# Windowed attention and routed experts on one core: the transfers of rows a step later, the splits of W2's sums one by one, table operations out of five products

## The chip, the core and the metric

The kernel runs on one core of one Trainium2 chip. The metric is device time in microseconds (us): the median of several executions of the whole program. One execution was also recorded by the hardware profiler. Its record, the trace, gives the start and length of every instruction on the core's engines, and all rows quoted here are from it. The engines are TensorE (PE; its weight loads are PEld), VectorE (DVE), ScalarE (ACT), GpSimd (POOL) and SyncE (SP, which issues most DMAs). Each works through its own instructions in order; semaphores hold an instruction until what it reads or overwrites is ready.

## What is computed

Attention over 8 batches, 8 heads, 576 positions and 64 dimensions, where each position sees itself and the 63 before it; then a mixture of 8 experts, of which each of the 4608 tokens takes the one with the largest logit:

```python
scores = np.matmul(q, k.transpose(0, 1, 3, 2)) / np.sqrt(64)
scores = np.where((rel >= 0) & (rel < 64), scores, -1e9)      # rel = row - column
attn = softmax(scores)
x = (attn @ v).transpose(0, 2, 1, 3).reshape(4608, 512)
logits = x @ w_gate + modality_bias[modality_id]
e_idx, gate_w = argmax(logits), max(softmax(logits))
for e in range(8):
    h = np.maximum(x[e_idx == e] @ w1[e], 0.0)                # 512 to 1024
    out[e_idx == e] = gate_w * (h @ w2[e])                    # 1024 to 512
```

## The kernel before

All loops are unrolled and the order of the instructions of every engine is written by hand: what the Python code issues first, an engine runs first.

**Steps.** The attention works on 36 pairs of blocks of 64 positions, 128 rows of x each. A loop over steps `s` (line 1211) runs 40 steps as a pipeline: step s computes the scores of pair s (`scores`, L748, on TensorE; `minima`, L765, the masked scores and their minimum per row on DVE; `exps`, L777, on ScalarE), turns the probabilities of pair s-1 (`probs_t`), multiplies pair s-2 with the values (`values`, L803; `values_out`, L811, which writes the pair's rows into a buffer `xa`) and takes the logits of pair s-3 (`logits`, L828, L833). A pair's own values and those of the block before it lie in different partitions, so `swap_v` puts a copy `ve` together: its upper half by DVE (L678), its lower by POOL (L679). POOL also adds a small number to the sums of the exponentials (`sums`, `rs`, L792), and in steps 6 to 11 makes the first half of a weight's split (`high`, L113).

**Rows.** Two pairs make a group G. In step 2G + 5, an odd one, `route2` and `route3` work out where each of the group's 256 tokens goes in a scratch memory that is sorted by expert. Small DVE operations wait in a list `routing`; `tick(n)` issues the next n of that list and then of a second list, `queue`, which holds table operations (on one partition, a few elements each: where an expert's rows begin, which experts are processed when). The last entry of `routing` is `rows`: a cast of the targets to integers (L916) and, for each of the two pairs, `scatter`: a POOL copy of the tokens' numbers into the last column of `xa` (L903) and an indirect DMA of the 128 rows of 514 numbers (L904). There are five `xa` buffers: pair p uses number p modulo 5. In steps 0 to 11 each step has ticks of 2, 6 and 6, from step 12 on of 2, 5 and 5. So up to step 11 the six entries behind `route3` all fit into the odd step's last tick; from step 12 on `rows` is left over, and runs at the next, even step's first tick, which stands behind that step's `swap_v`, `sums` and the transposes of x.

**Slots.** From step 12 on, pieces of the experts' work on TensorE stand between the parts of a step, and after step 39 they run alone. A slot is 256 tokens of one expert (`fetch` loads them from scratch into `xt`, L203; `x_part` turns them, L266, and splits them into `xh` and `xl`, L194 and L195). Numbers of 32 bits are split into a high and a low part, hi on ScalarE and lo on DVE, and three products are taken. From the eighth slot on, slots are "fast": the product with W2 takes seven half-size products P1 to P7 of sums and differences of its quarters (L387), in the order P1, P7, P2, P4, P5, P6, P3, with the first product's pieces (L291) between them.

**Sums of W2.** For this, `combine` (L1176, four POOL operations) makes the sums of two loaded pieces of W2, and `sums_parts` splits them (`put_parts`, L1179 on ScalarE and L1180 on DVE), three splits for the first expert, in steps 16 to 19, two for the second, in steps 36 to 39. `combine` runs in the middle of the step, behind `swap_v`; `sums_parts` at its end; the next pieces are loaded behind it (`sums_load`).

**After step 39** a loop (line 1509) issues the remaining pieces one by one and, after each, `tick(3)` until the table `rows2` is done and then `tick(1)`, as well as loads and splits of further weights.

Of the kernel before, what the change touches and what calls it, by code (L numbers as in the profile page):

```python
# [26 lines left out]
def tile_window_attn_moe(  # L27
# [12 lines left out]
    nc = tc.nc  # L40
    B, H, S, D = q.shape
    N = B * S
    DM = H * D
# [19 lines left out]
    FIRST = 12  # L63
# [144 lines left out]

    todo = []
    last = []  # L210
    position = [-4]
    pads = []
    RAWS = 8
# [22 lines left out]
    def run_later():  # L236
        while later:
            later.pop(0)()
# [14 lines left out]
    def slot_pieces():  # L253
# [157 lines left out]
        def fast_step(sl, nm):  # L411

            product(sl, nm, *dict(
                p1=("a11", "b11"), p7=("s3", "t3"), p2=("a12", "b21"), p4=("a22", "t4"),
                p5=("s1", "t1"), p6=("s2", "t2"), p3=("s4", "b22"))[nm])
            later.append(lambda: fast_out(sl, nm))
# [96 lines left out]
        while True:  # L513
            nxt = None
            if sl["fast"]:
                for k in (1, 2):
                    for i in range(2):
                        first(sl, k, i)
                        yield
                fast_step(sl, "p1")  # L520
                run_after()
                yield
                first(sl, 3, 0)
                yield
                nxt = fetch()
                first(sl, 3, 1)
                yield
                fast_step(sl, "p7")
                run_after()
                yield  # L530
                fast_step(sl, "p2")
                run_after()
                later.append(lambda: rest_of(sl, "s2"))
                yield
                fast_step(sl, "p4")
                later.append(lambda: rest_of(sl, "s4"))
                yield
                x_part(nxt, 0)
                run_later()
                x_part(nxt, 1)  # L540
                run_later()
                fast_step(sl, "p5")
                yield
                fast_step(sl, "p6")
                yield
                first(nxt, 0, 0)
                yield
                first(nxt, 0, 1)
                yield
                fast_step(sl, "p3")  # L550
                yield
                sl = nxt
                continue
            for k in range(1, NK):
                for i in range(2):
                    if k == 2 and i == 1:
                        assert todo
                        nxt = fetch()
                    first(sl, k, i)
                    yield  # L560
                for t in range(2):
                    second(sl, k - 1, t)
                    if k == NK - 1 and nxt and t == 1:
                        x_part(nxt, 1)
                    yield
                    if k == NK - 1 and nxt and t == 0:
                        x_part(nxt, 0)
                        run_later()
            second(sl, NK - 1, 0)
            yield  # L570
            if nxt["nb"] == 1:
                break
            first(nxt, 0, 0)
            yield
            first(nxt, 0, 1)
            yield
            second(sl, NK - 1, 1)
            yield
            sl = nxt
# [227 lines left out]
    def values_out(p):  # L807
        rs = st.pop((p, "rs"))
        nc.vector.reciprocal(out=rs, in_=rs)
        xa = st[p, "xa"] = xas[p % XBUF]  # L810
        nc.vector.tensor_tensor(  # L811
            out=xa[:, 0:DM].rearrange("p (h d) -> p h d", d=D), in0=st.pop((p, "av")),
            in1=rs[:, :, None].broadcast_to([P, H, D]), op=ALU.mult)

    def x_t(p, xp):
        xa = st[p, "xa"]
# [63 lines left out]
    def route3(G, rk):  # L880

        ex, oh = st.pop((G, "r")), chosen.pop(G)
        xg = [st.pop((GB * G + j, "xa")) for j in range(GB)]
        tgt = small.tile(sh3, F32, name="tgt")
        nc.vector.tensor_tensor(
            out=tgt, in0=rk.rearrange("p (j e) -> p j e", e=E), in1=ebase, op=ALU.add)
        se = small.tile([P, GB], F32, name="se")
        dst = small.tile([P, GB], F32, name="dst")
        idx = small.tile([P, GB], I32, name="idx")
        routing.append(lambda: nc.vector.reduce_sum(out=se, in_=ex, axis=AX.X))  # L890
        routing.append(lambda: nc.vector.tensor_tensor(out=tgt, in0=tgt, in1=oh[:, 1:], op=ALU.mult))
        routing.append(lambda: nc.vector.tensor_scalar(
            out=se, in0=se, scalar1=1e-9, scalar2=None, op0=ALU.add))
        routing.append(lambda: nc.vector.reduce_sum(out=dst, in_=tgt, axis=AX.X))

        def gates():
            for j in range(GB):
                nc.vector.reciprocal(out=xg[j][:, DM:DM + 1], in_=se[:, j:j + 1])
        routing.append(gates)

        def scatter(j):
            p = GB * G + j
            nc.gpsimd.tensor_copy(out=xg[j][:, DM + 1:DM + 2], in_=idc[:, p:p + 1])  # L903
            ins = nc.gpsimd.indirect_dma_start(  # L904
                out=xs, out_offset=bass.IndirectOffsetOnAxis(ap=idx[:, j:j + 1], axis=0),
                in_=xg[j], in_offset=None)
            tc.declare_no_dep(ins.ins, group="scatter", reason="rows are distinct")
            tc.add_to_no_dep_group("scatter", ins.ins)
            late = [T for T, _ in EARLY if T < G]
            if late:  # L910
                tc.declare_no_dep(ins.ins, group="early_loads", reason="rows read are older")
            for T in late:
                tc.add_to_no_dep_group(f"scatter_after_{T}", ins.ins)

        def rows():
            nc.vector.tensor_copy(out=idx, in_=dst)  # L916
            for j in range(GB):
                scatter(j)
            scattered.append(f"scatter_after_{G}")
        routing.append(rows)  # L920
# [257 lines left out]
    def put_parts(src, hi, lo):  # L1178
        nc.scalar.copy(out=hi, in_=src)  # L1179
        nc.vector.tensor_tensor(out=lo, in0=src, in1=hi.bitcast(F32), op=ALU.subtract)  # L1180
# [10 lines left out]
    def sums_load(x, j):  # L1191
# [2 lines left out]
            mixed[0][:, i * 512:(i + 1) * 512] for i in (2 * (j % 2), 2 * (j % 2) + 1)]  # L1194
        sums_x[x, j] = [load_piece(r, evs[x], 8 + j + 4 * i) for i, r in enumerate(raw)]

    def sums_parts(x, j):

        a, b = sums_x.pop((x, j))
        f13, f2 = combos[x][0:2]  # L1200
        put_parts(a, f13[0][:, j, :], f13[1][:, j, :])
        put_parts(b[:, half:DM], f2[0][:, j, :], f2[1][:, j, :])
        if not x:
            f4 = combos[x][2]
            put_parts(b[:, 0:half], f4[0][:, j, :], f4[1][:, j, :])

    combos = {}
    SUMS = {FIRST + 4 + j: (0, j) for j in range(4)}
# [2 lines left out]
    for s in range(NPR + 4):  # L1211
# [17 lines left out]
                       for _ in range(2)]))  # L1229
        for f, args in at.pop(s, ()):  # L1230
            f(*args)
        n_tick = 6 if s < FIRST else 5
        n_gap = 0 if s < FIRST else 4
        heads = list(parts[s])
        R = (s - 5) // GB if s >= 5 and j == 1 else -1
# [26 lines left out]
            high(s)  # L1262
        if s in SUMS:
            combine(*sums_x[SUMS[s]])
        if s < NPR:
            exps(s, (0, 1))
        if n_gap > 0 and s != FIRST:
# [3 lines left out]
        if 2 <= s < NPR + 2:  # L1271
            x_t(s - 2, turn_bank(s))
        run_later()
        tick(2)
        if s < NPR:
            exps(s, (2, 3, 4))
# [5 lines left out]
        if heads:  # L1282
            some_heads(s, *heads.pop(0), nc.vector.tensor_copy)
        run_later()
        tick(n_tick)
        cnt = None
        if R >= 0:
# [15 lines left out]
        while heads:  # L1303
# [2 lines left out]
                s, G, part, nc.scalar.copy if part in (K1, K0) or s < FIRST and (G, part) != (1, Q0) else  # L1306
                nc.vector.tensor_copy)
        run_later()
        tick(n_tick)
        if s >= 4:  # L1310
            weights(s)
        if s in SUMS:
            sums_parts(*SUMS[s])
        if s + 1 in SUMS:
            sums_load(*SUMS[s + 1])
        if n_gap > 3:
# [192 lines left out]
    while next(it, "end") != "end":  # L1509
        run_later()  # L1510
        t = position[0]
        waited += 1
        tick(3 if issued[0] < ready2 else 1)
        if len(pads) > E + 1:
            if t > begin_of[slot_y - 2]:
                pad_rows(pads.pop(0))
        elif len(pads) > E:
            if not todo or todo[0][2] != 0 or todo[0][1] is not None:
                pad_rows(pads.pop(0))
        elif pads and t >= begin_of[slot_y] + 16 and waited % 4 == 0:  # L1520
            tick(ready_i - issued[0], table=True)
            pad_rows(pads.pop(0))
        while n_load < len(loads) and loads[n_load][0] <= t + RAWS and (
                n_load < RAWS or loads[n_load - RAWS][3] < n_task):
            _, c, ev, _ = loads[n_load]
            raw_of[n_load] = load_piece(raw_tile(), ev(), c)
            n_load += 1
        if n_task < len(tasks) and tasks[n_task][0] <= t:
            _, f, ids = tasks[n_task]
            f(*(raw_of[i] for i in ids))  # L1530
            n_task += 1
# [125 lines left out]
```

## Time and profile before

| | us |
|---|---|
| median of 3 runs | 635.52 |
| lowest, highest | 634.42, 636.5 |
| the profiled execution | 640.02 |
| its span, first to last instruction | 638.2 |

The mean clock that TensorE was granted is 0.995 of full speed. In the profile, a row of the timeline gives an instruction's start and length in us, engine, line, operation, result and operands with their sizes, and, in brackets, how long the engine was idle before it and what ended that. `x32` means 32 such instructions merged into one row. `DVE xl L195` in a wait is the instruction of line 195 on DVE that writes `xl`. The step's number can be told from line 811, which each step has once: it begins step 7 at 53.68 us, step 9 at 65.50 and step 11 at 78.06.

### The profile page before, as it was taken

The page shows a single profiled execution, that of the slowest core. Times are in us where ns is not written, and L with a number is a line of the kernel's source. Part 1 is how long each engine was busy: PE and PEld are TensorE (multiplying, and loading weights), DVE is VectorE, ACT ScalarE, POOL GpSimd, SP SyncE. Part 2 cuts the span into 40 slices and gives each one's busy share as a digit, 9 for nine tenths or more (in the row PEclk, how much of TensorE's full clock was granted, in tenths as well). Part 3 has the DMA queues.
Part 4 walks back from the last instruction along what each step waited for, and adds up shares of the span by engine and source line. Part 5 has one row for each costly group of instructions (what it writes and reads, how often), then busy time and mean ns, then how long its engine had stood idle before and what let it go on. Part 6 is the DMA issues. An engine that isn't in the chain of part 4 may idle for free.

```text
span 638.2 us, 18317 instructions
## 1 busy us (share of the span) xinstructions
PE 611.9 (96%) x6831; PEld 567.1 (89%) x6831; DVE 431.9 (68%) x1645; ACT 340.4 (53%) x1049; POOL 177.1 (28%) x365
## 2 busy tenths in 40 slices
PE   6998889999999999999999989999999999999996
PEld 4887779888898989898988979999999999999885
DVE  2778967777757676666554567698667766675752
ACT  3799876666665656455644233463544454244541
POOL 5315431355232222320324650262111001101112
PEclk9999989999999999999999999999999999999999
DMA  9999884763754564534323347014773102505630
GB/s 178 194 186 244 217 226 124 207 191 85 199 166 123 151 160 134 140 79 115 102 78 115 97 156 236 34 49 133 238 243 117 51 34 67 181 18 187 210 118 35
DMA packets 141035, 89.71 MB, mean 141 GB/s; under 512 B 118858, under 2 KB 118896, under 8 KB 140784
## 3 DMA queue, kind: packets, MB, share of 16 engines
q1 hardware_dynamic: 132256, 69.02, 42.1%
q0 software_dynamic: 5856, 18.92, 7.8%
q8 instruction: 54, 0.88, 0.6%
q10 hardware_dynamic: 2832, 0.59, 0.5%
q14 instruction: 37, 0.30, 0.2%
HBM read 69.06 MB, written 24.96 MB: 147 GB/s over the span
## 4 chain that ended last, share of the span: by engine, by line
PE 55%; DVE 6%; DMA 1%; issue 1%; ACT 1%; POOL 1%; POOLq 0%; SPq 0%; DVEq 0%; ACTq 0%
PE em L291 14%; PE sp L291 9%; PE y L428 9%; PE y L387 7%; PE tp L608 4%; PE sp L387 3%; PE av L803 2%; PE sp L748 2%; PE av L387 2%; PE y L482 1%; PE tp L828 1%; DVE M L1180 1%; DVE y L407 1%; DMA vo<-in_moe_w_dram 1%; PE tp L266 1%
## 5 line engine op out<-in xcount | busy, mean ns | idle before, releaser
L777 ACT ACTIVATE ss<-ss,mn 128x128 f32<-128x128 f32 x240 | 94.1, 398 | 2.6 <-DVE mn L765 2.6
L442 POOL DMA_INDIRECT out_dram<-y,id x36 | 36.6, 1016 | 207.8 <-DVE y L407 114.4
L428 PE MATMUL y<-M,hh 128*128 128x512 f32 x256 | 83.6, 408 | 0.0
L291 PE MATMUL em<-xh,M 128*128 128x256 f32 x544 | 80.3, 290 | 2.4 <-DVE xl L195 2.4
L786 ACT COPY pT<-tp 128x512 f32<-128x512 f32 x59 | 32.5, 590 | 79.2 <-PE tp L608 78.1
L291 PEld LDWEIGHTS em<-xh,M 128*128 128x128 f32 x544 | 69.4, 191 | 3.3 <-DVE xl L195 3.1
L765 DVE CUSTOM_DVE_ANT_0 ss<-sp,masks 128x128 f32<-128x128 f32 x240 | 53.6, 287 | 19.6 <-PE sp L748 15.5
L904 POOL DMA_INDIRECT xs_scratch<-xa,idx x36 | 36.3, 1009 | 64.7 <-DVE rows L141 30.8
L428 PE MATMUL y<-M,hl 128*128 128x512 f32 x128 | 50.3, 393 | 0.0
L803 PEld LDWEIGHTS av<-ve,pT 128*64 128x64 f32 x576 | 36.3, 138 | 15.8 <-issue 9.5
L428 PEld LDWEIGHTS y<-M,hh 128*128 128x128 f32 x256 | 43.8, 188 | 6.0
L803 PE MATMUL av<-ve,pT 128*64 128x64 f32 x576 | 41.0, 225 | 6.5 <-DVE ve L678 3.3
L304 DVE SCALAR_TENSOR_TENSOR hl<-em,hh 128x512 fp32r<-128x512 f32 x32 | 22.1, 691 | 37.1 <-ACT hh L303 32.2
L777 ACT ACTIVATION_READ_ACCUMULATOR ss<-ss,mn 128x1 f32 x240 | 46.4, 193 | 0.0
L748 PE MATMUL sp<-kT,qT 64*64 64x128 f32 x1152 | 42.0, 284 | 2.2 <-DVE qT L731 0.8
L291 PE MATMUL em<-xl,M 128*128 128x256 f32 x272 | 43.4, 282 | 0.0
L291 PEld LDWEIGHTS em<-xl,M 128*128 128x128 f32 x272 | 37.0, 190 | 0.0
L291 PE MATMUL em<-xh,S 128*128 128x256 f32 x256 | 35.4, 280 | 0.8 <-DVE xl L195 0.7
L748 PEld LDWEIGHTS sp<-kT,qT 64*64 64x64 f32 x1152 | 32.5, 137 | 3.8 <-ACT qT L714 1.2
L291 PE MATMUL sp<-xh,S 128*128 128x256 f32 x256 | 35.2, 279 | 0.0
L803 PE MATMUL av<-vo,pT 128*64 128x64 f32 x480 | 34.4, 225 | 0.0
L608 PE MATMUL tp<-ident_r,ss 128*128 128x128 f32 x220 | 32.2, 284 | 1.8 <-DVE lg L833 1.8
(341 smaller groups left out, 1608.1 us busy)
## 6 DMA issues: line engine op xcount, KB each, us to landing
xt<-xs_scratch SPq DMA_DIRECT2D x18, 514.0 KB
vo<-in_v_dram SPq DMA_DIRECT2D x27, 256.0 KB
vo<-in_moe_w_dram SPq DMA_DIRECT2D x25, 256.0 KB
ss<-in_moe_w_dram SPq DMA_DIRECT2D x25, 256.0 KB
y<-in_moe_w_dram SPq DMA_DIRECT2D x24, 256.0 KB
xs_scratch<-xs_scratch SPq DMA_DIRECT2D x10, 514.0 KB
qk<-in_q_dram SPq DMA_DIRECT2D x16, 256.0 KB
qk<-in_k_dram SPq DMA_DIRECT2D x16, 256.0 KB
```

The source lines that it names most:

```text
L291: nc.tensor.matmul(out=hb[:, i * TP:(i + 1) * TP], lhsT=wap(buf, w, c0, P), rhs=x[:, c * TP:(c + 1) * TP], start=(n == 0), stop=(n == len( ...
L304: nc.vector.scalar_tensor_tensor(out=hl, in0=hb, scalar=0.0, in1=hh.bitcast(F32), op0=ALU.max, op1=ALU.subtract)))
L387: nc.tensor.matmul(out=out_, lhsT=w, rhs=factors[sl["buf"]][b][y](c), start=(m == 0), stop=(m == len(mm) - 1))
L428: nc.tensor.matmul(out=sl["y", t], lhsT=h[:, i * TP + t * P:i * TP + (t + 1) * P], rhs=wap(buf, w, c0, DM), start=(k == 0 and n == 0), sto ...
L442: ins = nc.gpsimd.indirect_dma_start(out=out, out_offset=bass.IndirectOffsetOnAxis(ap=sl["id"][:, t:t + 1], axis=0), in_=y, in_offset=None ...
L608: nc.tensor.transpose(out=out_, in_=in_, identity=ident[p0:p0 + n, p0:p0 + n])
L748: nc.tensor.matmul(out=sp[a][c * W64:(c + 1) * W64, hp * P:(hp + 1) * P], lhsT=qT[rows, g // GBLK, hp, g % GBLK + c], rhs=blocks(hp, g, g ...
L765: nc.vector.tensor_tensor_reduce(out=ss[a][:, hp, :], in0=sp[a][:, hp * P:(hp + 1) * P], in1=mask, scale=-1.0 / 8.0, scalar=3.0e38, op0=AL ...
L777: nc.scalar.activation(out=ss[a][:, hp, :], in_=ss[a][:, hp, :], func=AF.Exp, bias=mn[:, h:h + 1], scale=-1.0, accum_out=sm[:, h:h + 1])
L786: nc.scalar.copy(out=pT, in_=pp)
L803: nc.tensor.matmul(out=av[c * W64:(c + 1) * W64, 2 * hp + a], lhsT=pT[:, i:i + W64], rhs=(vo if c else ve)[p][:, 2 * hp + a, :], start=Tru ...
L904: ins = nc.gpsimd.indirect_dma_start(out=xs, out_offset=bass.IndirectOffsetOnAxis(ap=idx[:, j:j + 1], axis=0), in_=xg[j], in_offset=None)
```

## The change

Three things are changed.

1. Up to step 11 an odd step's ticks have five entries in place of six, so that `rows` is left to the next step's first tick there too. The copy of the tokens' numbers moves from `scatter` to `values_out`, right behind the writing of the pair's `xa`; in its place in `scatter` stands a memset of one element, as `send` has it ahead of its indirect DMA.
2. `sums_parts` no longer issues the splits but puts them into a list `spread`, right behind `combine`. A step issues those that stood in the list when it began, one at each of up to three places: ahead of its first tick, ahead of its second and ahead of its third. So they run a step later. What is left after step 39 is issued by the loop behind it, one after each piece.
3. In that loop no table operations are issued after the pieces from P2 to P6 of a fast slot (`dense`). After the others it is `tick(2)` in place of `tick(1)` once `rows2` is done.

```diff
@@ slot_pieces, the fast slot
                 fast_step(sl, "p7")
                 run_after()
                 yield
+                dense[0] = True
                 fast_step(sl, "p2")
...
                 fast_step(sl, "p6")
                 yield
+                dense[0] = False
                 first(nxt, 0, 0)
@@ values_out
             in1=rs[:, :, None].broadcast_to([P, H, D]), op=ALU.mult)
+        nc.gpsimd.tensor_copy(out=xa[:, DM + 1:DM + 2], in_=idc[:, p:p + 1])
@@ scatter
             p = GB * G + j
-            nc.gpsimd.tensor_copy(out=xg[j][:, DM + 1:DM + 2], in_=idc[:, p:p + 1])
+            nc.gpsimd.memset(pause, 0.0)
             ins = nc.gpsimd.indirect_dma_start(
@@ sums_parts
+    spread = []
     def sums_parts(x, j):
         a, b = sums_x.pop((x, j))
         f13, f2 = combos[x][0:2]
-        put_parts(a, f13[0][:, j, :], f13[1][:, j, :])
-        put_parts(b[:, half:DM], f2[0][:, j, :], f2[1][:, j, :])
+        spread.append(lambda: put_parts(a, f13[0][:, j, :], f13[1][:, j, :]))
+        spread.append(lambda: put_parts(b[:, half:DM], f2[0][:, j, :], f2[1][:, j, :]))
         if not x:
             f4 = combos[x][2]
-            put_parts(b[:, 0:half], f4[0][:, j, :], f4[1][:, j, :])
+            spread.append(lambda: put_parts(b[:, 0:half], f4[0][:, j, :], f4[1][:, j, :]))
+
+    def next_part():
+        if spread:
+            spread.pop(0)()
@@ the loop over steps
-        n_tick = 6 if s < FIRST else 5
+        late_parts = len(spread)
+        n_tick = 6 if s < FIRST and not j else 5
...
         if s in SUMS:
             combine(*sums_x[SUMS[s]])
+            sums_parts(*SUMS[s])
...
         run_later()
+        if late_parts > 2:
+            next_part()
         tick(2)
...
         run_later()
+        if late_parts > 1:
+            next_part()
         tick(n_tick)
...
         run_later()
+        if late_parts > 0:
+            next_part()
         tick(n_tick)
         if s >= 4:
             weights(s)
-        if s in SUMS:
-            sums_parts(*SUMS[s])
@@ the loop behind the steps
         waited += 1
-        tick(3 if issued[0] < ready2 else 1)
+        next_part()
+        if not dense[0]:
+            tick(3 if issued[0] < ready2 else 2)
```

In the diff, `FIRST` is 12, and `j` is 0 in even steps and 1 in odd ones.

More of the change, by code (lines that the diff above doesn't have):

```diff
@@ L210, in tile_window_attn_moe @@
     last = []
+    dense = [False]
     position = [-4]
```

## The prediction

> **What bounds the kernel now.** The engine table of the page comes first, then the waits of TensorE, longest total first (line that waited <- line that released it: us in total, times, longest).
>
> ```profile
> PE 611.9 (96%) x6831; PEld 567.1 (89%) x6831; DVE 431.9 (68%) x1645; ACT 340.4 (53%) x1049; POOL 177.1 (28%) x365
> ```
>
> ```profile
> PE av L803 <- DVE ve L678: 3.3, 5, 0.8
> PE tp L608 <- DMA qk<-in_k_dram: 3.2, 2, 1.8
> PE em L291 <- DVE xl L195: 3.1, 3, 1.4
> PE tp L608 <- DVE lg L833: 1.8, 4, 0.5
> ...
> PE av L803 <- POOL rs L792: 1.0, 1, 1.0
> ```
>
> TensorE is busy for 611.9 of 638.2 us, so at most 26.3 us can be gained anywhere, and only where TensorE waits. The busy time by stretch (columns: stretch, then busy us of PE, PEld, DVE, ACT, POOL, PE clock, DMA share, GB/s) tells steps 6 to 12 from the rest of the attention loop:
>
> ```profile
> 44.90:94.66 49.76, 42.12 (x775) 38.05 (x776) 40.93 (x223) 42.87 (x165) 21.41 (x39) 0.97 0.85 227
> 94.66:372.60 277.94, 275.29 (x3462) 247.30 (x3458) 181.93 (x840) 156.46 (x540) 90.75 (x166) 1.00 0.49 135
> ```
>
> The first loses 7.6 us of TensorE in 50, the second 2.7 in 278. A delay of any engine on the loop is therefore paid in full up to step 12, and mostly swallowed behind it.
>
> **Part 1, the rows.** Up to step 11 the `rows` entry (an index cast on DVE, two POOL operations, two indirect DMAs) leaves the end of an odd step and runs in the next even step behind DVE's `ve` copy; on POOL it passes behind that step's `ve` copy, `rs` sum and weight split. The timeline of DVE shows the loop (start, us, line, operation):
>
> ```profile
> 50.34 0.42 DVE L678 COPY ve<-S 64x512 f32<-64x512 f32 x1
> ...
> 53.68 0.69 DVE L811 TENSOR_TENSOR xa<-av,rs 128x512 f32<-128x512 f32 x1
> ...
> 62.20 0.42 DVE L678 COPY ve<-vo 64x512 f32<-64x512 f32 x1
> ...
> 65.50 0.69 DVE L811 TENSOR_TENSOR xa<-av,rs 128x512 f32<-128x512 f32 x1
> ...
> 74.21 0.42 DVE L678 COPY ve<-vo 64x512 f32<-64x512 f32 x1
> ...
> 78.06 0.69 DVE L811 TENSOR_TENSOR xa<-av,rs 128x512 f32<-128x512 f32 x1 [0.33 <-PE sp L748]
> ```
>
> These are steps 6 to 7, 8 to 9 and 10 to 11. The `xa` that an odd step 2G+7 writes is the buffer of pair 2G (five buffers, so five pairs later), and pair 2G's rows are now read out of it by a DMA issued in the step just before. Until now that DMA was a step older. When does it land? From the cast to the DMA's start, from start to landing, and what a wait for it looks like:
>
> ```profile
> 57.98 0.15 DVE L916 CAST idx<-dst 128x2 int32<-128x2 f32 x1
> ```
>
> ```profile
> 58.92 1.07 POOL L904 DMA_INDIRECT xs_scratch<-xa,idx  x1 [4.38 <-DVE rs L809]
> ```
>
> ```profile
> 345.06 0.75 DVE L436 TENSOR_SCALAR y<-y,gate 128x512 f32<-128x512 f32 x1 [1.75 <-PE y L428]
> ```
>
> ```profile
> 346.09 1.08 POOL L442 DMA_INDIRECT out_dram<-y,id  x1 [3.84 <-DVE lm L847]
> ```
>
> ```profile
> DMA to landing us min/median/max: 3.6/3.7/3.7
> ```
>
> ```profile
> 265.15 1.00 POOL L904 DMA_INDIRECT xs_scratch<-xa,idx  x1 [0.28 <-POOL xa L903]
> ```
>
> ```profile
> 269.56 0.69 DVE L811 TENSOR_TENSOR xa<-av,rs 128x512 f32<-128x512 f32 x1 [0.54 <-DMA xs_scratch<-xa,idx]
> ```
>
> Behind a copy, as before, the transfer starts 58.92 - 58.13 = 0.8 us after the cast's end. Behind the one-element memset that `send` uses, it starts 346.09 - 345.81 = 0.28 us after the data. The changed `scatter` has that memset, so I take 0.28 and keep 0.8 as the other end. Landing is 3.6 us after the start (the rows up to 200 us). The last pair shows that DVE does wait for this buffer, and there 4.4 us went from start to release: that end is kept too. The stall: `ve` ends at 50.76, the cast at about 50.95, the DMA starts at 51.23, lands at 54.83, DVE goes on at 54.88. Without the wait `xa` would start at 53.74 (53.68 and 0.06 for the cast): **1.14 us**. Step 9: 62.62 gives 66.74 against 65.56, **1.18 us**. Step 11: 74.63 gives 78.75 against 78.06, **0.69 us**. Behind the waiting `xa` on DVE stand the logits' sum, eight minima and the next `ve` copy, which TensorE awaits already:
>
> ```profile
> 56.73 0.24 PE L803 MATMUL av<-ve,pT 128*64 128x64 f32 x1 [0.66 <-DVE ve L678]
> ```
>
> `ve` ended at 56.58, TensorE went on 0.15 us later; so the stalls are paid in full: **+3.0 us**. Behind step 12 a step is long enough (277.94 us for some 26 of them) and nothing new waits. The moved index copy waits on POOL for the same landing, with the `ve` copy, the `rs` sum and the split behind it; TensorE wants that `ve` copy 3 us later, at 56.73 + 1.14, and no row shows one of them over 1.1 us: 0. What goes: POOL's `ve` copies behind the rows. TensorE's one wait marked POOL `rs`, of 1.0 us, comes right behind DVE's `ve` that ends at 50.76, so that copy was last anyway: I take 0; the other end is those 1.0 us gained. On SP the first load of rows waits for the transfers of G = 2:
>
> ```profile
> 78.50 0.39 SPq L203 DMA_DIRECT2D xt<-xs_scratch  x1
> ```
>
> ```profile
> 83.65 0.54 PE L266 MATMUL em<-ident_r,xt 128*128 128x128 f32 x4
> ```
>
> It would be issued near 80.1 instead of 78.50 (second transfer at 76.5 and 3.6), while TensorE's use slips only by step 11's 0.69: at most 0.9 us late if the load took all of the 5.15 us. I take 0. Fewer table entries per odd step cost nothing, the same ones run a step later.
>
> **Part 2, the splits of W2's sums.** Three waits hang on them. The last step of the loop, TensorE and then ScalarE:
>
> ```profile
> 370.75 0.46 PE L266 MATMUL tp<-ident_r,xt 128*128 128x128 f32 x4
> ...
> 372.25 0.39 PE L428 MATMUL y<-M,hl 128*128 128x512 f32 x1
> 374.04 1.21 PE L291 MATMUL em<-xh,M 128*128 128x256 f32 x8 [1.40 <-DVE xl L195]
> ```
>
> ```profile
> 371.17 0.62 ACT L1179 CAST kT<-vo 128x512 fp32r<-128x512 f32 x1 [3.78 <-POOL vo L1176]
> ...
> 372.31 0.58 ACT L194 CAST xh<-em 128x512 fp32r<-128x512 f32 x1
> ```
>
> The last split sits in front of the split of the next rows and waits for POOL's combining. Put behind the loop, `xh` and `xl` run as soon as TensorE's transposes end (370.75 and 0.46, 371.2): 0.6 us for `xh` (its row) and the 0.7 of a DVE pass over 128x512 bring 372.5, before 372.64 when TensorE is free. **-1.40 us**; next late is nothing. The two splits then fall where ScalarE idles for TensorE; if that cover were gone they would cost their 1.0 us. In steps 17 and 18, DVE and then TensorE:
>
> ```profile
> 147.85 2.71 DVE L1180 TENSOR_TENSOR S<-S,S 128x512 fp32r<-128x512 f32 x3
> ...
> 150.76 0.69 DVE L811 TENSOR_TENSOR xa<-av,rs 128x512 f32<-128x512 f32 x1
> ```
>
> ```profile
> 151.67 0.63 PE L608 MATMUL tp<-ident_r,ss 128*128 128x128 f32 x4 [0.49 <-DVE lg L833]
> ```
>
> ```profile
> 162.72 0.66 PE L608 MATMUL tp<-ident_r,ss 128*128 128x128 f32 x4 [0.39 <-DVE lg L833]
> ```
>
> Three splits at the step's end push `xa` and the logits' sum back. One of three remains there: **-0.49 and -0.39**. The other splits go between exponentials, where TensorE waited for nothing; between 0 and -0.88, I take the whole. The loads of the next sums on SP wait for splits half a step later; their combining has a step of room. In steps 36 to 39 as many splits as before stand ahead of the rows: 0.
>
> **Part 3, table operations.** TensorE's wait in the third fast slot, and its stretch:
>
> ```profile
> 441.15 1.10 PE L291 MATMUL em<-xh,S 128*128 128x256 f32 x7 [0.70 <-DVE xl L195]
> ```
>
> ```profile
> 419.00:441.20 22.20, 21.50 (x185) 21.28 (x183) 21.50 (x67) 10.27 (x24) 12.73 (x15) 1.00 0.23 76
> ```
>
> DVE is full for 22 us. I count some 30 table operations from 411 to 441; at two per piece outside P2 to P6, 14 more run before 411, and 9 fewer in the full stretch: at some 0.1 us each more than the 0.70. **-0.70 us** (between 0 and -0.70).
>
> **The sum**: +3.0 - 1.40 - 0.88 - 0.70 = 0.0 on the profiled execution, 640.02 us with its span of 638.2. The runs' median is 635.52, 4.5 us below it; carried over, **635.5 us**.
>
> **Rivals.** (a) *The rows land late*, the slower side: every 0.1 us more until landing costs 0.3 us over three stalls. With 4.4 us it is +2.4, with a start of 0.8 another +1.5: 637.9 to 639.4. It decides from 0.65 us more on. For: DMA share 0.85 there, and the 4.4 row. Against: 3.6 to 3.7 in just this stage. (b) *No stall*, if the transfer is free of the buffer earlier: -3.0, 632.5 us. Against it stands the row at 269.56; for it, that a landing 1.1 us sooner would do the same.
>
> The Trainium skill, DMA: Bandwidth & Descriptors, Anatomy of one DMA, gives 2.0 us and the bytes at 436 GB/s; for 128 rows of 2056 bytes that is an estimate of 2.6 us, and the stalls would fall to 0.3 in all, 632.8 us, next to (b). The trace does not agree, with 3.6.
>
> (c) *The clock drops* in the longer pauses:
>
> ```profile
> 88.00:90.00 2.00, 1.35 (x8) 1.36 (x9) 1.97 (x6) 2.00 (x9) 0.00 (x0) 0.79 0.61 178
> 90.00:92.00 2.00, 2.00 (x11) 2.00 (x11) 1.37 (x6) 2.00 (x10) 0.00 (x0) 0.50 0.26 64
> 92.00:94.00 2.00, 2.00 (x23) 1.87 (x23) 0.00 (x0) 1.75 (x7) 0.23 (x1) 0.86 0.30 70
> ```
>
> ```profile
> 52.41 1.10 PE L748 MATMUL sp<-kT,qT 64*64 64x128 f32 x32
> ```
>
> ```profile
> 88.64 1.69 PE L291 MATMUL em<-xh,M 128*128 128x256 f32 x8 [1.05 <-DVE xl L195]
> ```
>
> The missing clock is 0.42 + 1.00 + 0.28 = 1.7 us, after 5.0 us (83.65 to 88.64) with transposes and idling only. From the scores' end in step 7 to the next values (53.51 to 56.73) such a pause lasts 3.2 us and keeps the clock; it would grow to 4.4, between the two. Two drops give +3.4, 638.9 us.
>
> The Trainium skill, TensorE: Matmul & The Clock Gate, Part 1, lets an idle window of about 3.4 us halve the clock; the pauses of 3.2 us here did not, so the trace allows it.
>
> (d) *The gains stay away* because the splits push other work: +3.0, 638.5 us.
>
> **How the numbers follow.** Forecast 0.38 (own range 633.9 to 637.4), (a) 0.17, (b) 0.22, (c) 0.13, (d) 0.10. Runs tell about 0.3%, 1.9 us, from no change. Faster: 0.22 of (b) and 0.02 of the forecast's edge. Slower: 0.17 of (a), 0.09 of (c), 0.06 of (d), 0.04 of the edge. Same: 0.40. The range, 632.3 to 639.2, takes in (b), most of (a) and (c).
>
> **What would show it.** `xa` of steps 7, 9 and 11 waiting for the transfer by about 1.1, 1.2 and 0.7 us, and the span up to the start of step 12 about 3 us later; no such wait, and (b) holds. At the last step no `xl` wait of 1.4, in steps 17 and 18 no wait for `lg`, and none for `xl` near 441. A second clock slice under 1.00 shows (c). I am wrong above all if the buffer's wait is not where I put it.

## The result, and the profile after

The change makes the kernel slower, and by more than the range of the prediction allowed.

| | before | after |
|---|---|---|
| median, us | 634.97 | 643.40 |
| lowest, highest | 634.40, 636.50 | 641.72, 644.62 |
| ratio, with its 95% interval | | 1.0127 (1.0094 to 1.0161) |
| the profiled execution, its span | 640.02, 638.2 | 641.72, 639.9 |

The two profiled executions differ by 1.7 us, the medians by 8.4. So the profile of before was a long execution and that of after the shortest of its four; the experiments come back to this.

The busy time by stretch of the kernel after (columns as in the prediction: stretch, its length, then busy us of PE, PEld, DVE, ACT, POOL, the clock, DMA share, GB/s):

```profile
44.90:94.66 49.76, 37.20 (x702) 32.95 (x697) 35.91 (x209) 36.88 (x142) 17.73 (x40) 0.97 0.77 199
94.66:372.60 277.94, 276.25 (x3499) 248.99 (x3500) 182.87 (x840) 161.00 (x560) 93.59 (x193) 1.00 0.51 139
```

In the first stretch TensorE now loses 12.6 us of 49.8, where it lost 7.6. In the second it loses 1.7 where it lost 2.7. From `xa` of step 13 to the end of the span the kernel after takes 538.6 us (from 101.30), the first profile of before 542.9 (from 95.31). So the loss is in steps 6 to 12 and the gain behind them, as the prediction placed both. The longest waits of TensorE, and then DVE's wait for the row transfers from 44.9 to 100 us:

```profile
PE av L806 <- DVE ve L681: 3.3, 5, 0.8
PE tp L611 <- DVE xa L814: 3.3, 2, 2.7
PE em L611 <- DVE xa L814: 3.2, 1, 3.2
PE y L611 <- DVE xa L814: 3.2, 2, 3.0
...
PE em L292 <- DVE xl L195: 1.3, 2, 1.0
...
PE tp L611 <- DVE lg L837: 1.1, 3, 0.5
```

```profile
DVE xa L814 <- DMA xs_scratch<-xa,idx: 10.5, 3, 3.6
```

Three rows for `xa` are new. TensorE waits 9.7 us in all for what DVE writes into `xa`, and DVE waits 10.5 us, in three waits, for the row transfer to let go of that buffer. The timeline shows where (DVE, then POOL, which issues the transfers):

```profile
49.33 0.17 DVE L920 CAST idx<-dst 128x2 int32<-128x2 f32 x1
55.22 0.69 DVE L814 TENSOR_TENSOR xa<-av,rs 128x512 f32<-128x512 f32 x1 [3.42 <-DMA xs_scratch<-xa,idx]
...
69.28 0.69 DVE L814 TENSOR_TENSOR xa<-av,rs 128x512 f32<-128x512 f32 x1 [3.49 <-DMA xs_scratch<-xa,idx]
...
84.90 0.69 DVE L814 TENSOR_TENSOR xa<-av,rs 128x512 f32<-128x512 f32 x1 [3.61 <-DMA xs_scratch<-xa,idx]
```

```profile
49.80 1.22 POOL L908 DMA_INDIRECT xs_scratch<-xa,idx  x1 [1.61 <-DVE lm L851]
51.33 1.20 POOL L908 DMA_INDIRECT xs_scratch<-xa,idx  x1 [0.21 <-issue]
55.15 0.19 POOL L817 COPY xa<-idc 128x1 f32<-128x1 f32 x1 [2.62 <-DMA xs_scratch<-xa,idx]
...
63.77 1.07 POOL L908 DMA_INDIRECT xs_scratch<-xa,idx  x1 [2.79 <-DVE lm L851]
...
79.15 1.07 POOL L908 DMA_INDIRECT xs_scratch<-xa,idx  x1 [4.11 <-DVE lm L851]
```

The waits stand at steps 7, 9 and 11, where they were forecast. The cast ends at 49.50 and the transfer starts 0.30 us later, as forecast. What is different is the landing, which sets the buffer free: from the first transfer's start to `xa` it is 55.22 - 49.80 = 5.4 us, 69.28 - 63.77 = 5.5 and 84.90 - 79.15 = 5.75, where 3.6 had been taken.

### The profile page after: what moved, and what is told of

Read it like the earlier page. It is cut to its first block, busy times and chain, and to the rows that moved or that the text cites. A ratio compares the mean times of both kernels' runs of the same rounds, so it can differ in the third digit from the quotient of the medians.

```text
span 639.9 us, 18337 instructions
## 1 busy us (share of the span) xinstructions
PE 611.8 (96%) x6831; PEld 567.0 (89%) x6831; DVE 431.4 (67%) x1645; ACT 340.7 (53%) x1049; POOL 180.0 (28%) x401
## 4 chain that ended last, share of the span: by engine, by line
PE 58%; DVE 4%; issue 1%; ACT 1%; POOL 0%; POOLq 0%; DVEq 0%; ACTq 0%
PE em L292 15%; PE y L429 10%; PE sp L292 9%; PE y L388 7%; PE tp L611 4%; PE sp L388 3%; PE av L806 2%; PE av L388 2%; PE sp L751 2%; PE y L483 1%; PE tp L832 1%; PE tp L267 1%; PE em L267 1%; DVE M L1184 1%; DVE y L408 1%
## 5 line engine op out<-in xcount | busy, mean ns | idle before, releaser
L908 POOL DMA_INDIRECT xs_scratch<-xa,idx x36 | 37.6, 1044 | 52.5 <-DVE e_n_p L153 27.6
L814 DVE TENSOR_TENSOR xa<-av,rs 128x512 f32<-128x512 f32 x36 | 24.9, 691 | 20.8 <-DMA xs_scratch<-xa,idx 10.5
```

What stands on the lines that cost most here:

```text
L814: nc.vector.tensor_tensor(out=xa[:, 0:DM].rearrange("p (h d) -> p h d", d=D), in0=st.pop((p, "av")), in1=rs[:, :, None].broadcast_to([P, H ...
L908: ins = nc.gpsimd.indirect_dma_start(out=xs, out_offset=bass.IndirectOffsetOnAxis(ap=idx[:, j:j + 1], axis=0), in_=xg[j], in_offset=None)
```

## The experiments

One theory stood against three rivals. The theory: the loss is the buffer's wait, long because a row lands late. The rivals: parts 2 and 3 lose as well, POOL's queue loses, or TensorE's clock does. All ratios are against the kernel before in the same session. Its median was 636.65 us for e1 to e4, 639.17 for e5 to e8 and 638.95 for e9 to e12, each group on another chip, so only ratios can be compared across these groups.

| kernel | median, us | ratio | 95% interval |
|---|---|---|---|
| before, again (e1) | 636.87 | 1.0008 | 0.9995 to 1.0022 |
| part 1 alone (e2, e9) | 650.26, 648.48 | 1.0219, 1.0147 | 1.0196 to 1.0242, 1.0121 to 1.0173 |
| parts 2 and 3 (e3, e11) | 633.33, 636.11 | 0.9954, 0.9954 | 0.9937 to 0.9971, 0.9935 to 0.9974 |
| after, again (e5, e10) | 645.42, 645.02 | 1.0103, 1.0095 | 1.0066 to 1.0139, 1.0069 to 1.0121 |
| after, ten buffers (e4) | 635.76 | 0.9989 | 0.9975 to 1.0003 |
| the same, rows of G = 2 early (e8) | 636.14 | 0.9966 | 0.9946 to 0.9985 |
| parts 2 and 3, ten buffers (e12) | 634.37 | 0.9933 | 0.9910 to 0.9956 |
| after, pad transfer earlier (e6) | 644.17 | 1.0084 | 1.0055 to 1.0113 |
| after, TensorE kept busy (e7) | 646.16 | 1.0113 | 1.0088 to 1.0139 |

### Before, once more

> The kernel before, once more. Its profiled execution was 640.02 us while its runs' median is 635. If that execution was only a long one, this one's span is 633 to 635 us, with some stretch of 4 to 5 us gone against the first, and step 7 to 13 as in the first (xa of step 13 near 95.3 us behind the same landmarks): the comparison of the two profiles then hid 4 us of the 8.4 that the medians differ by. If instead profiles are always longer than plain runs by that much, the profile of after (641.7) would stand for 637, which its medians of 643 contradict.

Its span is 634.3 us, 3.9 below the first. The same stretches in this execution:

```profile
44.90:94.66 49.76, 42.74 (x791) 38.52 (x779) 42.73 (x233) 42.84 (x163) 21.91 (x40) 1.00 0.89 235
```

The clock is 1.00 where the first profile had 0.97 and its three slow slices at 88 to 94. From `xa` of step 6 to `xa` of step 13 this execution takes 47.36 us (44.20 to 91.56) and the first one 49.05 (46.26 to 95.31), so 1.7 of the 3.9 us are lost there. Another 2.1 are lost earlier, up to `xa` of step 6 (46.26 against 44.20). The second finding weighs more. Here is, first of the kernel before as it was predicted from and then of this execution, the row of the view of DMAs for the eight row transfers of steps 5 to 11 (the last number is the median time to landing), and under it the landing times from the view of that scratch memory:

```profile
xs_scratch<-xa,idx POOLq DMA_INDIRECT x8, 3.6
DMA to landing us min/median/max: 3.6/3.6/3.6
```

```profile
xs_scratch<-xa,idx POOLq DMA_INDIRECT x8, 6.2
DMA to landing us min/median/max: 4.5/6.2/7.3
```

The 3.6 with equal minimum, median and maximum is not eight equal transfers. Asked for each of the eight alone, the first trace has a landing for one only, the second transfer of step 7 (started at 60.47); for the other seven the view answers with no landing at all. Their packets are in the first trace, though. The 160 packets of the two transfers started at 47.01 and 48.71 run from 48.5 us to 54.1, so the second cannot have landed before 5.3 us; those of step 7 were all gone by 63.5, so the one landing that was seen is a short one. The execution of e1 has all eight, from 4.5 to 7.3 us. Even the early rows are awaited in it:

```profile
44.95 1.21 POOL L904 DMA_INDIRECT xs_scratch<-xa,idx  x1 [4.22 <-DVE xa L811]
```

```profile
52.40 0.69 DVE L811 TENSOR_TENSOR xa<-av,rs 128x512 f32<-128x512 f32 x1 [1.57 <-DMA xs_scratch<-xa,idx]
```

In this execution the step of slack that the kernel before has is thus 1.6 us too short for a landing of 7.3 us. The change gives up most of that slack.

### Part 1 alone

```diff
-        n_tick = 6 if s < FIRST else 5
+        n_tick = 6 if s < FIRST and not j else 5
...
+        nc.gpsimd.tensor_copy(out=xa[:, DM + 1:DM + 2], in_=idc[:, p:p + 1])
...
-            nc.gpsimd.tensor_copy(out=xg[j][:, DM + 1:DM + 2], in_=idc[:, p:p + 1])
+            nc.gpsimd.memset(pause, 0.0)
```

> Only part 1 (rows a step later up to step 11, memset for the copy, index copy behind xa). Theory, the wait for the rows' landing (three waits of 3.4 to 3.6 us at xa of steps 7, 9 and 11, partly taken back by shorter even steps) costs all of the 8.4 us and parts 2 and 3 gain up to 3: +8 to +11.5 us against before, 643 to 646.5. Rival, parts 2 and 3 are themselves a loss: +5 to +6, near 640.5.

> Part 1 alone once more, beside the kernel after. So far it stood at 1.0219 of before and the kernel after at 1.0103 to 1.0127, though parts 2 and 3 are worth only 0.0046. Theory (the length of a landing, and with it whether the clock falls in the pause, differs from execution to execution and session to session, in both kernels alike): the two differ by 0.003 to 0.007 here, part 1 alone at 1.014 to 1.019. Rival (part 1 alone has something of its own that costs 3 to 4 us more): 1.020 or more, with the clock of the stage at 0.84 again.

It came out 13.6 us above before in the one session and 9.5 in the other, so the first expectation was missed on the high side and the second was met. DVE's wait for the rows, in e2 and in e9:

```profile
DVE xa L814 <- DMA xs_scratch<-xa,idx: 13.4, 3, 5.0
```

```profile
DVE xa L814 <- DMA xs_scratch<-xa,idx: 11.8, 3, 5.0
```

In e2 the clock also fell, to 0.84 over the stage; e9 (columns as above, another stretch) shows 0.97:

```profile
44.90:94.66 49.76, 36.91 (x621) 32.93 (x618) 32.41 (x190) 34.07 (x137) 17.36 (x37) 0.84 0.68 180
```

```profile
44.90:96.00 51.10, 39.96 (x714) 34.47 (x711) 36.37 (x212) 37.11 (x143) 17.76 (x40) 0.97 0.70 185
```

All four executions of e2 have a mean clock of 0.979 to 0.984, those of e9 0.996 or 0.997; the last section of the experiments puts a price on that. Part 1 carries the whole loss, and more than the whole.

### Parts 2 and 3 without part 1

The edit is the rest of the change: the rows as before, with the index copy in `scatter`.

> Parts 2 and 3 without part 1. Theory (their gains are real as priced, 1.40 + 0.88 + 0.70): -3.0 us at most, 632 to 633.5, with no xl wait at the last step, none of 0.70 near 441 and no two lg waits in steps 17 and 18. Rival, the gains stay away or they cost: 635 or more.

> Parts 2 and 3 alone once more, for comparison within this call: 0.994 to 0.997 of before, 2 to 4 us.

Both runs give 0.9954, some 2.9 us, and neither interval reaches 1. TensorE's waits from 105 to 600 us, first in e1 and then in e3:

```profile
PE em L291 <- DVE xl L195: 2.1, 2, 1.4
PE tp L608 <- DVE lg L833: 1.7, 4, 0.5
PE em L266 <- DMA xt<-xs_scratch: 0.7, 1, 0.7
```

```profile
PE tp L611 <- DVE lg L836: 0.9, 2, 0.5
PE em L267 <- DVE qT L1183: 0.5, 1, 0.5
PE sp L388 <- DVE bias_sel L141: 0.5, 1, 0.5
PE em L292 <- DVE xl L195: 0.3, 1, 0.3
```

Waits of 4.5 us have become 2.2. The sum that was forecast, -2.98, is about what was measured, and 633.33 lies in the expected range; the terms are not all the forecast ones. The waits for `xl` of 1.4 and 0.7 are gone and the waits for `lg` are halved. New are a wait behind a split (`qT`, 0.5) and one behind a table operation:

```profile
429.64 0.39 PE L388 MATMUL sp<-M,hl 128*128 128x256 f32 x1 [0.52 <-DVE bias_sel L141]
```

The profile names the table operation that ended at that moment. What the product reads is `hl`, which ended 0.06 us before:

```profile
428.91 0.67 DVE L346 SCALAR_TENSOR_TENSOR hl<-sp,hh 128x512 fp32r<-128x512 f32 x1
```

Between the `hl` before it (at 424.48) and this one DVE runs six table operations and takes 4.43 us; in e1 it is three, and 3.52 us (425.81 to 429.33). The table operations that part 3 takes out of P2 to P6 gather between the other pieces, and there they now stand in front of what TensorE needs. With this wait and the one for `xl` that is left, 0.27 at 412.41 us, the rows show nothing that remains of part 3's 0.70. The waits account for 2.3 us of the 2.9; the rest lies within the intervals. Parts 2 and 3 were not run apart, so the split between them is a reading of rows.

### The kernel after, again

> The kernel after, once more, beside e1 to e4: part 1 alone came out at 650.3 us where the kernel after, which does nothing else in the first 150 us, had 643.4 in its own session, though parts 2 and 3 are worth only 3.3 (e3). If chips or sessions differ in how long a row transfer lands, this comes out at 646 to 648 here, with more slices of a clock under 1.00 in 55 to 100 us than the first profile of it had (one of 2.9 us near 86); if parts 2 and 3 are worth more behind part 1, it stays at 643.

> The kernel after a third time, for comparison within this call: 1.010 to 1.013 of before; xa of steps 7, 9 and 11 waits 2.6 to 4.5 us each.

The ratios are 1.0103 and 1.0095, a little under the 1.0127 of the first measurement and inside its interval. The second lies just below its expected range; its three waits, 4.03, 4.06 and 3.18 us, lie in theirs. In the last session part 1 alone stood at 1.0147, parts 2 and 3 at 0.9954: +1.47 and -0.46 make +1.01%, and 0.95 was measured. The parts add up there. With the 1.0219 of e2 they would not, but the kernel after was not run in e2's session.

### Ten buffers

Pairs 5 to 9 write their `xa` into a stretch of a weight buffer that held `v` of the first pairs, each part of it already used, and that is free until step 15. No row transfer of these steps is then in the way of a later `xa`; the order of the program stays as after the change.

```diff
-        xa = st[p, "xa"] = xas[p % XBUF]
+        xa = st[p, "xa"] = (
+            stock[2][:, (p - XBUF) * ROW:(p - XBUF + 1) * ROW] if XBUF <= p < 2 * XBUF else xas[p % XBUF])
```

> The kernel after, with the xa of pairs 5 to 9 in a free stretch of a weight buffer, so that no row transfer of the steps up to 12 is awaited by a later xa. Theory (the buffer's wait is the loss): no xa wait in steps 7, 9 and 11, and the time falls below before by the gains of parts 2 and 3, 632 to 634 us. Rival 1, the loss is POOL's queue (index copies and rs, ve copies behind the rows) or the order on DVE: the waits turn into others and it stays at 638 to 643. Rival 2, TensorE's clock in the pauses: as rival 1, with clock slices under 1.0 in 44 to 95 us.

The loss is gone, from 1.0103 or 1.0095 to 0.9989, and DVE no longer waits for rows in this stage. The landings are as long as before: the five of eight that its trace has took 5.5 to 7.4 us. That is the test of the theory: the same order, the same POOL queue, transfers as slow, and only the shared buffer taken away. (POOL's index copies waited for the same buffer, so the run does not part their wait from DVE's; in the kernel after, TensorE's waits name `xa`.) But it does not reach the 0.9954 of parts 2 and 3, nor the 632 to 634 us expected. TensorE's longest waits from 40 to 100 us in it, and the row behind the second:

```profile
PE av L806 <- DVE ve L681: 3.3, 4, 1.0
PE em L267 <- DMA xt<-xs_scratch: 3.0, 1, 3.0
```

```profile
84.83 0.51 PE L267 MATMUL em<-ident_r,xt 128*128 128x128 f32 x4 [3.04 <-DMA xt<-xs_scratch]
```

The load of `xt` must wait for the rows of G = 2. Its cost had been put at 0, at most 0.9; here it is 3.0. From `xa` of step 6 to that of step 13 this execution takes 48.92 us and e3 46.45, 2.5 less, which is about the difference of the two ratios. In the kernel after the wait for `xt` hides behind the waits for `xa`.

In the next kernel step 9 has its six entries again, so the rows of G = 2 leave early:

```diff
-        n_tick = 6 if s < FIRST and not j else 5
+        n_tick = 6 if s < FIRST and (not j or s == 9) else 5
```

> As the run with ten buffers, but the rows of G = 2 leave at the end of step 9 as before; those of G = 0 and 1 a step later. In the run with ten buffers the load of xt (issued at 80.69 instead of 76.60) made TensorE wait 3.0 us and the clock fell to 0.56 to 0.59 for 4 us: its loss of 2.4 us against parts 2 and 3 alone. Theory (that wait is the whole of it): 1 to 2 us under parts 2 and 3 alone, 631 to 633, and no wait of TensorE for xt. Rival (the rest of it is the POOL queue or noise): 634 to 636.

The wait for `xt` is gone from this kernel's trace and the ratio is 0.9966: nearer to parts 2 and 3 alone, not below them as expected. With nothing colliding, issuing the rows later gains nothing that can be seen.

Last, parts 2 and 3 with early rows and ten buffers:

> Parts 2 and 3, rows at the end of the odd steps as before, and the xa of pairs 5 to 9 in the free stretch. In the usual execution of before (e1) the xa of step 7 waited 1.57 us for the rows although they left a step earlier, since they landed 7.4 us after the first transfer's start. Theory (landings of 5 to 7 us touch even the early rows of step 7): 0.3 to 1.5 us under parts 2 and 3 alone, 0.992 to 0.996. Rival (that wait is covered by others): the same as parts 2 and 3 alone.

0.9933 is the lowest ratio of all. Its interval, to 0.9956, overlaps that of parts 2 and 3 alone (0.9935 to 0.9974), so whether the buffers add to the gain is open. Both beat the kernel before and the kernel after.

### What makes the landing long, and the clock

> The kernel after, with the transfer of the pad rows (514 KB, issued at 64.50 us, 0.7 us behind the first row transfer of step 8) moved from the end of step 9 to the end of step 7 in the program. Theory, rows land late because SP's loads and the pad run on the same DMA engines at that moment: the wait of xa in step 9 (3.49 us) falls to 1.2 to 2.2, that of step 11 stays at 3.6, and the time by 1 to 2 us. Rival, the row transfers need 5.5 us by themselves from this place on: the wait of step 9 stays within 0.3 us of 3.5.

```diff
-        if s == 9:
+        if s == 7:
             ins = nc.sync.dma_start(out=xs_blk[DUMMY:DUMMY + 2].rearrange("b p c -> p b c"), in_=padrow)
```

The wait of step 9 was 3.81 us, inside what the kernel after shows there (3.49, 4.32 and 4.06 in its three profiles). The rival's side: that 514 KB transfer, which now starts at 57.37, is not what delays the rows. The view of DMA queues of the kernel after shows where a landing's time goes, for the first row transfer of step 8 in two stretches (63.77 to 66.10 and 66.10 to 68.20 us; packets, MB, share of the DMA engines; q0 holds the rows, q1 what SP issues), and then for the first one of step 12, which starts at 95.87 (95.87 to 97.40, 97.40 to 98.50):

```profile
q1 hardware_dynamic: 1115, 0.42, 67.1%
...
q1 hardware_dynamic: 297, 0.57, 72.3%
q0 software_dynamic: 81, 0.27, 31.4%
```

```profile
q1 hardware_dynamic: 644, 0.16, 46.5%
...
q0 software_dynamic: 80, 0.26, 76.2%
q1 hardware_dynamic: 51, 0.01, 5.1%
```

Step 8: 2.3 us without a packet of the rows, 2.1 us for their 80 packets beside SP's loads at 72%, and another 1.1 until DVE goes on at 69.28. Step 12, with almost nothing beside it once they move: 1.5, 1.1 and 0.7 (POOL goes on at 99.21), 3.3 in all. That the traffic beside them stretches each part is what these two pairs of rows suggest. But the second transfer of step 12 started 1.4 us behind the first and took 4.9, and the run with the pad moved speaks against it for the last part. Here is the same view of that run, for 66.10 to 68.20 us and then for 68.20 to 69.66, where DVE goes on:

```profile
q0 software_dynamic: 150, 0.49, 60.2%
q1 hardware_dynamic: 122, 0.17, 23.7%
...
q0 software_dynamic: 9, 0.03, 5.9%
q1 hardware_dynamic: 2, 0.00, 0.4%
```

Beside a third of the traffic (24% in place of 72%), 150 of the 160 packets of both transfers are through by 68.20, where the kernel after had 81. Still the landing is no earlier: 69.66 - 63.83 = 5.8 us. Nine packets follow one by one over the last 1.5 us with next to nothing beside them. Their 5.9% of sixteen DMA engines is the time of about one engine (an estimate: 0.059 x 16 = 0.94), so it looks as if one engine were still working off its share while the others are done. Why, no run has shown; nor what fills the 2.3 us ahead of the first packet.

> The kernel after, with eight dummy products (128x512, of zeros) on TensorE ahead of the transposes of x in steps 7, 9 and 11, where it waits for the rows. Theory of the pauses (part of the loss is the granted clock that falls in the longer pauses): no slice under 1.00 between 44 and 100 us and 1 to 4 us less than the kernel after, with the waits of xa unchanged at 3.4 to 3.6. Rival, the clock costs nothing because TensorE waits there anyway: the same time within 0.5 us.

```diff
-            x_t(s - 2, turn_bank(s))
+            xp = turn_bank(s)
+            if s in (7, 9, 11):
+                for _ in range(8):
+                    nc.tensor.matmul(out=xp, lhsT=idle[:, 0:P], rhs=idle[:, 0:512], start=True, stop=True)
+            x_t(s - 2, xp)
```

The same stretch of e5, the kernel after in that session, then of e7, and of the run with the pad moved (e6):

```profile
44.90:96.00 51.10, 41.42 (x712) 35.98 (x709) 37.60 (x215) 38.04 (x147) 17.96 (x40) 0.93 0.77 198
```

```profile
44.90:96.00 51.10, 42.92 (x732) 35.09 (x735) 35.45 (x211) 36.15 (x140) 17.71 (x40) 1.00 0.73 188
```

```profile
44.90:96.00 51.10, 39.27 (x704) 33.86 (x700) 37.16 (x212) 38.27 (x148) 18.43 (x41) 1.00 0.76 196
```

In e7 the clock stayed at 1.00 and the time did not fall: 1.0113 against 1.0103. But DVE's waits for the rows were 13.4 us in this execution, so a gain could be hidden in this comparison. The run with the pad moved is a cleaner one. Its clock was 1.00 as well, DVE's waits were the 10.5 us of the first profile of after (clock 0.97), and from `xa` of step 6 to that of step 13 the two take 55.72 and 55.74 us. So at a clock of 0.97 the fall costs nothing that can be seen.

In e2 it does cost: the same steps take 61.52 us there, and 57.89 in e7, with 13.4 us of waits in both (parts 2 and 3, which e2 lacks, act behind this stage). The 3.6 us are what the clock of 0.83 to 0.84 costs, as far as two executions can tell; it is most of the 4.9 by which e2 is longer than e9 (56.65).

## Why the prediction was wrong

**Where the loss sits: right.** The waits are at `xa` of steps 7, 9 and 11, for the buffer five pairs older, with the transfer 0.3 us behind the cast. That the stalls are paid in full held nearly: DVE waits 8.9 us more than in e1 (10.5 against 1.6), and steps 6 to 13 take 8.4 more. Rival (b), no stall, fell with the first profile.

**How long it is: wrong, and this is the step that failed.** The sentence is "Landing is 3.6 us after the start (the rows up to 200 us)". With 5.4, 5.5 and 5.75 us in its place, the stalls of 1.14, 1.18 and 0.69 grow by 1.8, 1.9 and 2.1, from 3.0 to 8.8 us. DVE waited 10.5. The rest is that DVE reached `xa` earlier than reckoned: in step 7 it stood idle from 51.80 us (55.22 - 3.42), 2.5 us after its `ve` copy's end at 49.29, where 53.74 - 50.76 = 3.0 had been taken. In step 9 it is 2.5 in place of 2.9, in step 11 2.6 in place of 3.4: 1.7 us in all. So the term "+3.0" for part 1 measured 8.4. By the start of `xa` of step 13 the kernel after is 8.4 us behind (45.56 to 101.30 is 55.74; e1 has 47.36).

The 4.4 us of the row 265.15 to 269.56 had been kept as the other end and was still too short. Rival (a), the rows land late, is what happened: it had the mechanism and its point of decision, 0.65 us more. Its upper end of 639.4 came from that 4.4, and its chance of 0.17 from the trust in 3.6. The argument against it, "3.6 to 3.7 in just this stage", rested on two transfers, and the second of them, started at 133.8 us, is not of this stage.

The Trainium skill, DMA: Bandwidth & Descriptors, Anatomy of one DMA, led to an estimate of 2.6 us for such a transfer. The traces do not agree: 3.3 us for the first transfer of step 12, 4.5 to 7.3 in the busy stage of e1.

**The costs put at 0.** POOL's index copies waited 9.1 us as well, 8.1 of them for the same three landings and at the same time, and with ten buffers the order on POOL did no harm that could be seen. The `xt` load was worth 3.0, not 0 to 0.9, once nothing covered it.

**Parts 2 and 3: right in sum, in part by luck.** -2.98 was forecast, 0.9954 measured twice. Of the terms, -1.40 and the `lg` waits held by and large. Part 3's -0.70 was taken back by new waits. The waits make up 2.3 us and the rest was not placed, so that the sum fits so well is partly luck. Rival (d), the gains stay away, fell.

**The clock, rival (c).** It does fall behind the longer pauses, to 0.84 over the stage in e2 and to 0.93 in e5, in slices of 2 us down to 0.50. In e2 such a slice stands behind each of TensorE's three waits for `xa`, of 3.7 to 4.1 us; in the kernel after behind the third, of 3.2, and not behind those of 2.7 and 3.0. The Trainium skill, TensorE: Matmul & The Clock Gate, Part 1, has the clock halved after an idle window of about 3.4 us. The fall to half agrees; the length cannot be read off these rows, as e5 has slices of 0.50 behind a wait of 2.1. As the cause of the loss of the kernel after it fell with e6 and e7; in part 1 alone, in the session of e2, it added to the loss.

**The base.** The profiled execution was 4 to 5 us longer than the usual one, and 1.7 us of the 3.9 against e1 lay in the stage in question. Carrying a difference over to the median was right; taking the stage's landings from that one execution was not.

## What to carry to other kernels

A median with equal minimum and maximum over eight transfers is a warning that few of them were seen: ask for each one, and where landings are missing, look for the queue's last packets instead. Before a transfer out of a buffer is issued later, compare the time left until that buffer is written again with the longest landing in the same stage, not with the typical one elsewhere; a step of slack that looks idle can be what the landings use. A change of several parts is worth measuring by parts: here a gain of 0.5% stood behind a loss three times its size.

## What was not expected of the hardware

The same transfer, 128 rows of 2056 bytes, landed in 3.3 us when SP's loads took 5% of the DMA engines while its packets moved, and in 4.5 to 7.3 us in the stage of e1, where the engines are 89% busy (the row of 44.90 to 94.66). Moving a neighbouring 514 KB transfer away let the packets through sooner and did not shorten the landing: the last nine packets of two transfers took 1.5 us with the queues else empty, at the pace of about one of the sixteen engines.
